# Fewer dummy matmuls, an on-chip broadcast for the last tile, folded output instructions and an early clock warm-up, in an attention + gated-MLP kernel

## Chip, cores, metric

One NeuronCore of one Trainium2 chip. The metric is device time in microseconds (us), median of several executions; lower is better. Engines are called PE (TensorE), ACT (ScalarE), DVE (VectorE), POOL (GpSimd), SP (SyncE, which issues the transfers).

## The reference, cut to what matters

```python
# S = 2048 rows, D = 448, 16 heads of 28, MLP width 1792, all bf16
def reference(x, wqkv, wo, w_gate, w_up, w_down, gate_w):
    g = sigmoid((x * gate_w).sum(-1, keepdims=True))
    q, k, v = split(x @ wqkv)
    a = concat_heads(softmax(q @ k.T * 28 ** -0.5) @ v) @ wo     # attention
    b = (gelu(x @ w_gate) * (x @ w_up)) @ w_down                 # gated MLP
    return g * a + (1 - g) * b
```

## The kernel before

Attention runs in 512 steps: 4 groups of heads, 4 tiles of 512 queries (so 16 tiles, numbered j), two pairs of heads p, 16 blocks of 128 keys. In each step PE computes two score blocks (one pair of heads, each on 32 rows of the array), ACT takes their exponential, and PE multiplies it with V (each head on 32 columns of the array). Between, PE gets "fillers": matmuls of the projections and of the MLP, two a step. Where no real work is ready, dummies are put in.

```python
FILL_BUDGET = [2, 2]
DUMMY_FILL = True
...
def emit_fillers(budget, allow_dummy=True):
    ...
        if j is None:                      # no job ready
            ...
            while n < budget:              # dummies: nobody reads the result
                kb.add("pe", lambda e, _s=dslot: e.matmul(_s.ap[:, 0:512], xT[0][0:128, 0:128],
                                                          xT[0][0:128, 0:512]))
                n += 1
            return
...
for i in range(NSTEP):
    if i + 1 < NSTEP: emit_S(i + 1)        # score pair of the next step
    emit_exp(i)                            # ACT
    emit_fillers((4 if i < EARLY_STEPS else FILL_BUDGET[i % 2]) + extra_fill.get(i, 0))
    emit_PV(i)                             # PV pair
    ...
```

After its 32 steps a tile is divided by the softmax denominators, which lie in one row in 32. For the last tile:

```python
def stage_last():
    Wdve(c_pv, last_pv)
    ... tensor_copy(den_sb, psO[obuf])          # DVE
    ... reciprocal(rrows, den_sb)               # DVE
    ... dma_start(bcast, rows of rrows to all)  # SP: one row to 32 partitions
    ... tensor_tensor(oT, den_sb, bcast, mult)  # DVE
```

Then four tiles of the output are still to be done; each has one matmul and

```python
v1 = tensor_tensor(tmpc[:, t % 2], psum, acc16[:, t], add)
Wdve(c_cb, v1)
if t >= 2: wait(d_out[t - 2])
v2 = scalar_tensor_tensor(outsb[:, t % 2], tmpc[:, t % 2], g16[:, t], b_sb[:, t], mult, add)
... dma_start(out rows, outsb[:, t % 2])
```

The softmax here doesn't subtract the row's maximum and nothing guards it: scores larger than these inputs give would overflow.

## Time and profile before

| | before |
|---|---|
| median (16 runs, with those beside the changed kernel) | 655.5 us |
| span of the profiled run | 654.7 us |
| first real matmul starts | 17.42 |
| first scores start | 30.82 |
| last PV seen complete by DVE | 634.25 |

The four instants cut the run into loading, projections (13.40 us), steps (603.43 us) and tail (20.45 us to the end of the span). They are read from the timeline. The lines themselves stand in the prediction. "Busy" of PE is not work done: matmuls are pipelined, each shows some 0.39 us though a new one can start every 0.216.

### The profile page before, as it was taken

The numbers are of one execution on the slowest core, as the hardware profiler recorded it, in microseconds if no ns is written. First come the engines' busy times: TensorE is split into PE (matmuls) and PEld (weight loads), VectorE is DVE, ScalarE is ACT, GpSimd is POOL, SyncE is SP. The second block draws the span as 40 slices with busy tenths as digits, with TensorE's granted clock in tenths as the row PEclk, the third lists the DMA queues.
The fourth block names the chain that finished last, engine by engine and source line by source line (L and its number), as shares of the span: only waits on it lengthen the run. The fifth ranks groups of instructions, "written<-read, shape, count | busy, mean of one in ns | idle before, by whom it ended". The sixth has DMA issues, their size and how long they took to land.

```text
span 654.7 us, 8803 instructions
## 1 busy us (share of the span) xinstructions
PE 615.3 (94%) x3145; PEld 165.6 (25%) x3145; DVE 311.4 (48%) x603; ACT 541.0 (83%) x542; POOL 11.0 (2%) x22
## 2 busy tenths in 40 slices
PE   0899999999999999999999999999999999999971
PEld 0332222222222222222222222222222222222210
DVE  4553578883154788217874721788111243112053
ACT  0067899999988999999998999999898899889860
POOL 6000000000000000000000000000000000000000
PEclk9999999999999999999999999999999999999995
DMA  8910000000000000000000000000000000100001
GB/s 198 295 29 1 1 18 1 17 2 10 8 2 18 2 17 2 14 5 2 18 1 19 1 17 1 3 17 0 18 1 18 1 10 23 31 10 26 13 28 44
DMA packets 21265, 15.34 MB, mean 23 GB/s; under 512 B 13544, under 2 KB 17832, under 8 KB 21224
## 3 DMA queue, kind: packets, MB, share of 16 engines
q1 hardware_dynamic: 21224, 14.80, 9.4%
q8 instruction: 25, 0.41, 0.3%
q14 instruction: 16, 0.13, 0.1%
HBM read 6.42 MB, written 1.84 MB: 13 GB/s over the span
## 4 chain that ended last, share of the span: by engine, by line
PE 92%; DVE 2%; DMA 2%; SPq 2%; ACT 2%; issue 0%; DVEq 0%
PE psO L792 25%; PE psS L764 25%; PE psY L445 9%; PE psX L445 9%; PE psX L682 6%; PE psY L524 4%; PE psX L524 4%; PE psX L271 2%; PE psY L271 2%; ACT pT L775 2%; SPq L219 1%; DMA bcast<-rrows 1%; PE psS L271 1%; PE psY L563 1%; PE psY L682 1%; PE psX L563 1%
## 5 line engine op out<-in xcount | busy, mean ns | idle before, releaser
L775 ACT ACTIVATE pT<-psS 128x1024 bf16<-128x1024 f32 x512 | 516.1, 1023 | 91.8 <-PE psS L764 76.7
L792 PE MATMUL psO<-pT,vext 128*32 128x512 bf16 x1024 | 201.1, 390 | 2.6 <-ACT pT L775 2.6
L764 PE MATMUL psS<-qT,kT 32*128 32x512 bf16 x1024 | 198.3, 384 | 0.9 <-DVE vext L324 0.9
L792 PEld LDWEIGHTS psO<-pT,vext 128*32 128x32 bf16 x1024 | 49.0, 92 | 206.5 <-issue 171.3
L764 PEld LDWEIGHTS psS<-qT,kT 32*128 32x128 bf16 x1024 | 47.9, 91 | 117.2 <-issue 112.9
L445 PE MATMUL psY<-xT,wg 128*128 128x512 bf16 x224 | 67.8, 384 | 0.0
L445 PE MATMUL psX<-xT,wu 128*128 128x512 bf16 x224 | 65.5, 383 | 0.0
L453 DVE CAST uS<-psX 128x512 bf16<-128x512 f32 x56 | 38.7, 692 | 52.0 <-PE psX L445 52.0
L682 PE MATMUL psX<-xT 128*128 128x512 bf16 x147 | 44.5, 384 | 0.0
L453 DVE CAST gS<-psY 128x512 bf16<-128x512 f32 x56 | 38.5, 688 | 2.7 <-PE psY L445 2.7
L489 DVE SCALAR_TENSOR_TENSOR gu<-gS,uS 128x512 bf16<-128x512 bf16 x56 | 38.3, 684 | 0.0
L513 DVE SCALAR_TENSOR_TENSOR hT<-tt,gu 128x512 bf16<-128x512 bf16 x56 | 35.9, 683 | 1.7 <-ACT tt L501 1.7
L531 DVE TENSOR_SCALAR bsb<-psY,omg 128x448 bf16<-128x448 f32 x8 | 5.5, 684 | 53.7 <-PE psY L524 53.7
L524 PE MATMUL psY<-wd,hT 128*128 128x448 bf16 x112 | 30.9, 358 | 0.0
L524 PE MATMUL psX<-wd,hT 128*128 128x448 bf16 x112 | 30.9, 358 | 0.0
L501 ACT ACTIVATE tt<-zt 128x1024 bf16<-128x1024 bf16 x28 | 29.3, 1048 | 0.0
L531 DVE TENSOR_SCALAR bsb<-psX,omg 128x448 bf16<-128x448 f32 x8 | 5.5, 684 | 41.0 <-PE psX L524 41.0
L483 DVE TENSOR_TENSOR zt<-ww,gS 128x512 bf16<-128x512 bf16 x56 | 23.8, 425 | 2.1
L838 DVE TENSOR_TENSOR oT<-densb,bcast 128x512 bf16<-128x512 f32 x15 | 10.3, 688 | 29.9 <-DMA bcast<-rrows 29.9
L473 DVE TENSOR_TENSOR x<-gS 128x512 bf16<-128x512 bf16 x56 | 23.3, 416 | 0.0
L445 PEld LDWEIGHTS psX<-xT,wu 128*128 128x128 bf16 x224 | 14.6, 98 | 25.6 <-issue 20.4
L587 DVE TENSOR_TENSOR tmpc<-psY,acc 128x448 bf16<-128x448 f32 x8 | 5.0, 624 | 32.2 <-PE psY L577 32.1
(88 smaller groups left out, 258.1 us busy)
## 6 DMA issues: line engine op xcount, KB each, us to landing
bcast<-rrows SPq DMA_DIRECT2D x16, 256.0 KB
out_dram<-outsb SPq DMA_DIRECT2D x16, 112.0 KB, 1.7
wd<-in_B_w_down_dram SPq DMA_DIRECT2D x1, 1568.0 KB, 15.6
wg<-in_B_w_gate_dram SPq DMA_DIRECT2D x3, 448.0 KB, 5.0
wu<-in_B_w_up_dram SPq DMA_DIRECT2D x3, 448.0 KB, 8.4
hT<-in_A_wqkv_dram SPq DMA_DIRECT2D x3, 336.0 KB, 3.5
wop<-in_A_wo_dram SPq DMA_DIRECT2D x16, 24.5 KB
sp<-densb SPq DMA_DIRECT2D x15, 8.0 KB
```

The lines of the kernel that those rows point to most:

```text
L271: return e.matmul(slot.ap[:, 0:512], wsrc[c][0:128, g, :, :], xT[c][0:128, tc * 512:(tc + 1) * 512], start=(c == 0), stop=(c == 3), tile_p ...
L445: e.matmul(s.ap[:, 0:512], _w[_c][0:128, _f * 128:(_f + 1) * 128], xT[_c][0:128, _tc * 512:(_tc + 1) * 512], start=(_c == 0), stop=(_c == ...
L453: v = kb.add("dve", lambda e, _s=s: e.tensor_copy(_dst[:, _k % 2, :], _s.ap[:, 0:512]), ctr=c_d)
L483: kb.add("dve", lambda e, _kp=kp, _mp=mp: e.tensor_tensor(zt[:, _mp, _kp, :], ww[:, :], gS[:, _kp, :], ALU.mult), ctr=c_d)
L489: kb.add("dve", lambda e, _kp=kp, _k4=k % 4: e.scalar_tensor_tensor(gu[:, _k4, :], gS[:, _kp, :], 0.5, uS[:, _kp, :], ALU.mult, ALU.mult), ...
L501: kb.add("act", lambda e, _mp=mp: e.activation(tt[:, :, :], zt[:, _mp, :, :], AF.Tanh, scale=TANH_C), ctr=c_th)
L513: kb.add("dve", lambda e, _kk=kk, _k4=k % 4, _f=f, _tc=tc: e.scalar_tensor_tensor(hT[:, _tc % 2, _f, :], tt[:, _kk, :], 1.0, gu[:, _k4, :] ...
L524: e.matmul(s.ap[:, 0:D], hT[:, _tc % 2, _f, _tl * 128:(_tl + 1) * 128], wd[:, _f, :], start=(_f == 0), stop=(_f == FC - 1), tile_position= ...
L682: kb.add("pe", (lambda e, _s=dslot: e.matmul(_s.ap[:, 0:512], xT[0][0:128, 0:128], xT[0][0:128, 0:512])))
L764: return e.matmul(psS[_buf][:, _hh * 512:(_hh + 1) * 512], kT2[_g % 2][32 * _hp:32 * _hp + 32, _kc * 128:(_kc + 1) * 128], qT2[_g % 2][32 ...
L775: kb.add("act", lambda e, _buf=buf: e.activation(pT[:, _buf, :], psS[_buf][:, 0:1024], AF.Exp, scale=SM_SCALE), ctr=c_exp)
L792: return e.matmul(psO[_obuf][32 * _hp:32 * _hp + 32, :], v_ext[:, _kc, _h, :], pT[:, _buf, _hh * 512:(_hh + 1) * 512], start=(_kc == 0), s ...
```

## The change

It has four parts: (1) where nothing is ready, one dummy a step in place of a full budget; (2) the last tile is normalised in two halves, one per pair of heads, in two PSUM banks, and the reciprocals are spread over partitions by a matmul with a block of ones (`e_bc`) in place of a DMA, with 18 dummies ahead of the second one (a maximum comes before each reciprocal, so that the rows that are no denominators, which the matmul multiplies by 0, stay finite); (3) the gate and the MLP's half are added when the accumulator is evacuated, so that an output tile needs one DVE instruction, with four output buffers; (4) 16 dummies at the start, once the first chunk of the transposed input is there.

```diff
+        kb.wait_sem("pe", d_xt[0], 16)                      # part 4
+        for _ in range(16):
+            kb.add("pe", lambda e: e.matmul(psY[:, 0:512], xT[0][0:128, 0:128], xT[0][0:128, 0:512]))
         Wpe(c_wp, WP_ALL)
...
-                v = ... e.tensor_copy(acc16[:, _t, :], _s.ap[:, 0:D])          # part 3
+                v = ... e.scalar_tensor_tensor(acc16[:, _t, :], _s.ap[:, 0:D],
+                        g16[:, _t:_t + 1], b_sb[:, _t, :], ALU.mult, ALU.add)
...
-                v1 = ... e.tensor_tensor(tmpc[:, _t % 2, :], _s.ap[:, 0:D], acc16[:, _t, :], ALU.add)
-                Wdve(c_cb, v1)
-                if _t >= 2: kb.wait_sem("dve", d_out[_t - 2], 16)
-                v2 = ... outsb[:, _t % 2, :] from tmpc, g16, b_sb
+                if _t >= 4: kb.wait_sem("dve", d_out[_t - 4], 16)
+                v2 = ... e.scalar_tensor_tensor(outsb[:, _t % 4, :], _s.ap[:, 0:D],
+                        g16[:, _t:_t + 1], acc16[:, _t, :], ALU.mult, ALU.add)
...
-                    while n < budget:                                          # part 1
+                    while n < 1:
...
-            def stage_last(): ...                                              # part 2
+        def emit_norm_last(pr, last_pv):      # pr = 0, 1; partitions 64*pr .. 64*pr+63
+            ... tensor_scalar(rrows, den_sb if pr == 0 else psO[obuf], 1e-30, max)
+            ... reciprocal(bcast, rrows)
+            ... (pr == 1: 18 dummies on PE)
+            ... matmul(slot, e_bc, bcast)     # fp32, 64 x 64 tile of the array
+            ... tensor_tensor(oT, den_sb, slot, mult)
```

More of the change, by code (lines that the diff above doesn't have):

```diff
@@ L126, in bass_gated_mix__mha_block__glu_gated_geglu__prompt_kernel @@
         den_sb = T("densb", [128, 512], F32)
+        e_bc = T("ebc", [128, 128], F32)
         sp16 = T("sp16", [128, 16], F32)
@@ L148, in bass_gated_mix__mha_block__glu_gated_geglu__prompt_kernel @@
         omg16 = T("omg16", [128, NT], F32)
-        tmpc = T("tmpc", [128, 2, D], BF16)
-        outsb = T("outsb", [128, 2, D], BF16)
+        outsb = T("outsb", [128, 4, D], BF16)
         psS = [P(f"psS{i}", [128, 1024]) for i in range(2)]
@@ L208, in bass_gated_mix__mha_block__glu_gated_geglu__prompt_kernel @@
         kb.add("pool", lambda e: e.memset(wu[3][0:64, :], 0.0), ctr=c_ms)
+        kb.add("pool", lambda e: e.memset(e_bc[:, :], 0.0), ctr=c_ms)
+        MS_E0 = c_ms.n
+        for hp in range(4):
+            kb.wait("pool", c_ms, MS_E0)
+            kb.add("pool", lambda e, _hp=hp: e.memset(e_bc[32 * _hp:32 * _hp + 1, 32 * _hp:32 * _hp + 32], 1.0), ctr=c_ms)
         MS_ALL = c_ms.n
@@ L568, in evac @@
             def evac(s, _t=t):
-                v = kb.add("dve", lambda e, _s=s: e.tensor_copy(acc16[:, _t, :], _s.ap[:, 0:D]), ctr=c_ae)
+                Wdve(c_be, BE_ALL_holder[0])
+                Wdve(c_g, gate_done["v"])
+                v = kb.add("dve", lambda e, _s=s: e.scalar_tensor_tensor(
+                    acc16[:, _t, :], _s.ap[:, 0:D], g16[:, _t:_t + 1], b_sb[:, _t, :], ALU.mult, ALU.add),
+                    ctr=c_ae)
                 acc_done[_t] = v
@@ L582, in evac @@
                 Wdve(c_ae, acc_done[_t])
-                Wdve(c_be, BE_ALL_holder[0])
-                Wdve(c_g, gate_done["v"])
                 if cb_last[0]:
                     Wdve(c_cb, cb_last[0])
-                v1 = kb.add("dve", lambda e, _s=s: e.tensor_tensor(
-                    tmpc[:, _t % 2, :], _s.ap[:, 0:D], acc16[:, _t, :], ALU.add), ctr=c_cb)
-                Wdve(c_cb, v1)
-                if _t >= 2:
-                    kb.wait_sem("dve", d_out[_t - 2], 16)
-                v2 = kb.add("dve", lambda e: e.scalar_tensor_tensor(
-                    outsb[:, _t % 2, :], tmpc[:, _t % 2, :], g16[:, _t:_t + 1], b_sb[:, _t, :],
+                if _t >= 4:
+                    kb.wait_sem("dve", d_out[_t - 4], 16)
+                v2 = kb.add("dve", lambda e, _s=s: e.scalar_tensor_tensor(
+                    outsb[:, _t % 4, :], _s.ap[:, 0:D], g16[:, _t:_t + 1], acc16[:, _t, :],
                     ALU.mult, ALU.add), ctr=c_cb)
@@ L597, in evac @@
                 kb.add("sp", lambda e: e.dma_start(
-                    out[0, _t * 128:(_t + 1) * 128, :], outsb[:, _t % 2, :]).then_inc(d_out[_t], 16))
-                return (c_cb, v1)
+                    out[0, _t * 128:(_t + 1) * 128, :], outsb[:, _t % 4, :]).then_inc(d_out[_t], 16))
+                return (c_cb, v2)
             j = Job(f"z{t}", mm_fns, evac)
@@ L747, in step_of @@
             return g, qc, p, kc
+        last_j = G * NTC - 1
+        nm_half = {}
+        bc_slot_free = [None]
         def emit_S(i):
@@ L781, in emit_PV @@
             obuf = j % 2
+            if j == last_j and p == 1:
+                obuf = 1 - obuf
             Wpe(c_exp, i + 1)
@@ L786, in emit_PV @@
                 Wpe(c_cp, j - 1)
+            if kc == 0 and p == 1 and j == last_j:
+                Wpe(c_cp, j)
             buf = i % 2
@@ L841, in stage2 @@
                 nm_val[j] = v
-            def stage_last():
-                Wdve(c_pv, last_pv)
-                kb.wait_sem("dve", d_spr, 16 * j)
-                Wdve(c_nm, j)
-                kb.add("dve", lambda e, _obuf=obuf: e.tensor_copy(den_sb[:, :], psO[_obuf][:, :]), ctr=c_cp)
-                cpv = c_cp.n
-                Wdve(c_cp, cpv)
-                kb.wait_sem("dve", d_bc, 16 * j)
-                kb.add("dve", lambda e: e.reciprocal(rrows[:, :], den_sb[:, :]), ctr=c_rc)
-                rcv = c_rc.n
-                Wsp(c_rc, rcv)
-                Wsp(c_nm, j)
-                kb.add("sp", lambda e: e.dma_start(
-                    bcast[:, :], bass.AP(rrows, 0, [[32 * 512, 4], [0, 32], [1, 512]])).then_inc(d_bc, 16))
-                kb.wait_sem("dve", d_bc, 16 * (j + 1))
-                v = kb.add("dve", lambda e, _g=g, _qc=qc: e.tensor_tensor(
-                    oT[_g][:, _qc * 512:(_qc + 1) * 512], den_sb[:, :], bcast[:, :], ALU.mult), ctr=c_nm)
-                nm_step[j] = step[0]
-                nm_val[j] = v
             if j == G * NTC - 1:
-                deferred.append((step[0] + 1, stage_last))
                 return
@@ L868, in emit_norm, with task, copy_out, pe_part @@
             deferred.append((step[0] + 15, stage2))
+        def emit_norm_last(pr, last_pv):
+            g = last_j // NTC
+            qc = last_j % NTC
+            obuf = last_j % 2
+            if pr == 1:
+                obuf = 1 - obuf
+            r0 = 64 * pr
+            def task():
+                Wdve(c_pv, last_pv)
+                if pr == 0:
+                    kb.wait_sem("dve", d_spr, 16 * last_j)
+                    Wdve(c_nm, last_j)
+                def copy_out():
+                    kb.add("dve", lambda e, _o=obuf, _r0=r0: e.tensor_copy(
+                        den_sb[_r0:_r0 + 64, :], psO[_o][_r0:_r0 + 64, :]), ctr=c_cp)
+                    Wdve(c_cp, c_cp.n)
+                if pr == 0:
+                    copy_out()
+                if pr == 0:
+                    kb.wait_sem("dve", d_bc, 16 * last_j)
+                kb.add("dve", lambda e, _r0=r0: e.tensor_scalar(
+                    rrows[_r0:_r0 + 64, :], (den_sb if pr == 0 else psO[obuf])[_r0:_r0 + 64, :], 1e-30, None, ALU.max), ctr=c_rc)
+                Wdve(c_rc, c_rc.n)
+                kb.add("dve", lambda e, _r0=r0: e.reciprocal(bcast[_r0:_r0 + 64, :], rrows[_r0:_r0 + 64, :]), ctr=c_rc)
+                rcv_half[pr] = c_rc.n
+                if pr == 1:
+                    copy_out()
+                if pr == 0:
+                    deferred.append((step[0] + 4, pe_part))
+                else:
+                    pe_part()
+            def pe_part():
+                rcv = rcv_half[pr]
+                slotb = fslots[pr % 2]
+                if slotb.free is not None:
+                    Wpe(slotb.free[0], slotb.free[1])
+                if pr == 1:
+                    for _ in range(18):
+                        kb.add("pe", lambda e, _s=slotb: e.matmul(
+                            _s.ap[:, 0:512], xT[0][0:128, 0:128], xT[0][0:128, 0:512]))
+                Wpe(c_rc, rcv)
+                Wpe(c_ms, MS_ALL)
+                bv = kb.add("pe", lambda e, _s=slotb, _r0=r0: e.matmul(
+                    _s.ap[_r0:_r0 + 64, 0:512], e_bc[_r0:_r0 + 64, _r0:_r0 + 64], bcast[_r0:_r0 + 64, :],
+                    tile_position=(_r0, _r0)), ctr=c_pv)
+                Wdve(c_pv, bv)
+                v = kb.add("dve", lambda e, _s=slotb, _r0=r0: e.tensor_tensor(
+                    oT[g][_r0:_r0 + 64, qc * 512:(qc + 1) * 512], den_sb[_r0:_r0 + 64, :],
+                    _s.ap[_r0:_r0 + 64, 0:512], ALU.mult), ctr=c_nm)
+                nm_half[pr] = v
+                slotb.free = (c_nm, v)
+                slotb.free_step = step[0]
+                if pr == 1:
+                    nm_step[last_j] = step[0]
+                    nm_val[last_j] = v
+            deferred.append((step[0] + 1, task))
@@ L870, in process_deferred @@
+        cp_half = [None]
+        rcv_half = {}
         def process_deferred():
@@ L888, in bass_gated_mix__mha_block__glu_gated_geglu__prompt_kernel @@
                 emit_norm(g * NTC + qc, c_pv.n)
+            if g * NTC + qc == last_j and kc == KC - 1:
+                emit_norm_last(p, c_pv.n)
             process_deferred()
```

## The prediction

> **What bounds the kernel now.** I read the page's first two parts first, then the chain that ended last in order of time, then the timeline at both ends. The page's head and its clock row say that TensorE (PE) is the engine to think about, and that its clock is full except in the last slice:
>
> ```profile
> PE 615.3 (94%) x3145; PEld 165.6 (25%) x3145; DVE 311.4 (48%) x603; ACT 541.0 (83%) x542; POOL 11.0 (2%) x22
> PEclk9999999999999999999999999999999999999995
> ```
>
> The middle of the chain, in order of time (start, us, piece), shows one attention step as a cycle on PE:
>
> ```profile
> 605.11 0.32 PE psO L792 x2
> 605.43 0.32 PE psS L764 x2
> 605.75 0.54 PE psX L682 x2
> 606.29 0.32 PE psO L792 x2
> ```
>
> A step is a pair of PV matmuls (L792), a pair of score matmuls (L764) and two fillers: 0.32 + 0.32 + 0.54 = 1.18 us. Here the fillers are dummies of L682, which compute nothing. Neighbouring matmuls of one kind start 0.216 us apart (the 16 warm ones below), so two take 0.43 and 0.11 goes to changing the array's tiling; the pairs, which run beside each other, cost 0.216 + 0.11 each. ScalarE (ACT) is not far behind. Where fillers are few, its exponentials run back to back, and there the chain changes to ACT (timeline: start, us, engine, group; then two PV rows of that stretch):
>
> ```profile
> 31.25 2.86 ACT L775 ACTIVATE pT<-psS 128x1024 bf16<-128x1024 f32 x3 [29.22 <-PE psS L764]
> ...
> 625.73 0.39 PE L792 MATMUL psO<-pT,vext 128*32 128x512 bf16 x2 [0.18 <-ACT pT L775]
> ...
> 629.42 0.39 PE L792 MATMUL psO<-pT,vext 128*32 128x512 bf16 x2 [0.18 <-ACT pT L775]
> ```
>
> Three exponentials of 1.02 in 2.86 us start (2.86-1.02)/2 = 0.92 apart; from 625.73 to 629.42 are four steps of 0.92. So ACT's floor is 0.92 us a step, PE's with two fillers 1.18.
>
> The two ends are serial (timeline of the first 31 us, and of the last 21):
>
> ```profile
> 4.85 10.12 SPq L219 DMA_TRANSPOSE xT<-in_A_x_dram  x4
> 17.42 1.86 PE L271 MATMUL psS<-xT,wqP 128*128 128x512 bf16 x4 [17.42 <-DMA xT<-in_A_x_dram]
> 23.68 1.03 PE L271 MATMUL psO<-xT,wkP 128*128 128x512 bf16 x4
> 30.82 0.60 PE L764 MATMUL psS<-qT,kT 32*128 32x512 bf16 x4 [0.94 <-DVE vext L324]
> 634.25 0.69 DVE L847 COPY densb<-psO 128x512 f32<-128x512 f32 x1 [4.28 <-PE psO L792]
> 634.98 3.35 DVE L851 RECIPROCAL rrows<-densb 128x512 f32<-128x512 f32 x1
> 645.29 0.69 DVE L858 TENSOR_TENSOR oT<-densb,bcast 128x512 bf16<-128x512 f32 x1 [6.96 <-DMA bcast<-rrows]
> 646.13 0.53 PE L577 MATMUL psY<-wop,oT 128*128 128x448 bf16 x1 [11.92 <-DVE oT L858]
> 651.79 0.69 DVE L592 SCALAR_TENSOR_TENSOR outsb<-tmpc,g,bsb 128x448 bf16<-128x448 bf16 x1
> ```
>
> At the start the first 16 projection matmuls take 6.43 us on the chain (17.42 to 23.85, 0.40 each) and the next four 0.86 (0.216 each): the first are cold. At the end, after the last PV (634.25), come copy, reciprocal, a 6.9 us DMA broadcast, multiply, and four output tiles each of two VectorE (DVE) instructions in series; the span ends at 654.7, so this tail is 20.4 us.
>
> **What the Trainium skill says.** "TensorE: Matmul & The Clock Gate", section "What's actually happening": PE runs at half clock until it has been busy for a window of about 3.4 us, with a free-running window. The trace agrees in direction (0.40 then 0.216 us) but shows 5 to 6 us of cold work. "TensorEngine Tiling (Array Packing)", "Key Properties": changing the tiling mode drains the array. The trace shows 0.11 us at each change; so one filler costs 0.216 + 0.11, and removing the second saves only 0.216. "VectorE: DVE Perf Modes", "The TRN2 errata": an fp32 tensor_tensor takes (N+151)/0.96 ns, 691 for 512; L858 agrees at 0.69. I use it to say that 64 partitions in place of 128 save no time. "FP8 and Floating Point Precision", "TensorE Precision Notes": true FP32 is four passes. No matmul in this trace is fp32; the new one I estimate at 4 x 0.216 = 0.86 us plus some 0.2 for drain.
>
> **Part 1, one dummy a step in place of two.** The order of both built programs' instructions, cut into the 512 steps at the PV pairs, gives: 80 steps with two dummies keep one; one step with four keeps one; three with one output matmul and one dummy lose the dummy; one loses both to the new broadcast matmul. 169 dummies become 81. All else in the steps is the same, in the same order. A step with one dummy has PE work of 3 x 0.32 = 0.966 us, still just above ACT's 0.92. The rest of its loop fits: scores start to exponential start is 0.43 us (624.22 to 624.65), the exponential 1.02, some 0.05 to the PV, 1.50 in all, where PE reaches that PV only five thirds of a cycle, 1.61 us, after the scores. So PE stays the bound, by little, and 80 x 0.216 = 17.3 us is saved. The three mixed steps fall from about 1.16 to the ACT floor, 3 x 0.2 = 0.6. The four-dummy step stands at a Tanh (1.05 us on ACT): two PE steps of 1.18 + 1.61 = 2.79 against three ACT instructions at 0.92 to 0.95, some 2.8; it and its neighbour gain nothing, -0.2. Sum 17.7.
>
> **Part 2, the last tile's normalisation in halves.** The first half's VectorE work (copy 0.69, maximum about 0.5, reciprocal 3.35, near 4.6 with gaps) starts after step 495 and lies beside four to five steps of 0.966; its broadcast matmul comes after PV of step 500, about 5.1 us later, so hardly a wait. The matmul is 0.86 to 1.0 us plus an added tiling change, in a step that loses two dummies of 0.54: about 0.5 us lost. The second half is the tail, counted from the last PV: maximum from PSUM 0.70, reciprocal to 4.1, broadcast matmul (0.86 + 0.2, the 18 dummies before it last 18 x 0.216 = 3.9 us and keep it warm without delaying it) to 5.3, multiply to 6.05; the copy of 0.69 hides beside the matmul. The first output matmul then gives its result by 6.6. Before, the same point (646.70) was at 12.45. Saved 5.85.
>
> **Part 3, one VectorE instruction per output tile.** Before, four tiles take 646.70 to 652.49 = 5.8 us, 1.48 a tile for the first three. After, one instruction of 0.69 and a wait between, 0.72: 4 x 0.72 = 2.9. Saved 2.9. The other instruction is not gone, it is folded into the accumulator's evacuation (0.625 becomes 0.685, 16 times), where VectorE idles between tiles. Four output buffers remove a wait that cost nothing (0.6 us of idle in all). The last store's 2.2 us stay. So the tail is 6.6 + 2.9 + 2.2 = 11.7 in place of 20.4: 8.7 saved in parts 2 and 3.
>
> **Part 4, 16 dummies at the start.** They wait only for the first transposed chunk, issued at 4.85 and landed 5.2 us later, at 10.05. Cold at 0.43 they end at 16.9, with some warm earlier; the real work begins at 17.42 as before, since the last chunk is still what it waits for. Then 16 matmuls take 3.46 us in place of 6.43; VectorE, at 0.87 a V tile against PE's 0.86, can follow. Saved 2.7 (estimate), if the gap of about 1 us does not cool the clock. The five added GpSimd memsets come after those that anything early waits for.
>
> **Sum.** 17.7 - 0.5 + 8.7 + 2.7 = 28.6. From 655.4: 626.8 us.
>
> **The rivals.** (a) The dummies' steps fall to ACT's floor: 80 x 0.04 = 3.5 us more, 623. For it: the drain could be partly overlapped where PE waits. Against it: the chain's 0.11 is in every cycle. (b) PE and ACT, now nearly equal, wait for each other in turn, and a step takes 1.02 (the exponential's full length) rather than 0.966: 80 x 0.05 = 4.3 us back, 631. For it: both buffers are only two deep; against it: exponentials 0.92 apart exist. (c) The dummies were what kept the clock full, and half as many let it fall: each dummy step would go to about 1.7 us or more, 80 x 0.7 = 56 us, some 680. Against it: stretches with one or no filler (624.8 to 630) keep matmuls at 0.39 and the clock row at 9. (d) The early dummies do not warm it, or overrun: the 2.7 is lost, 629.5. (e) The fp32 matmul or the DVE queue at step 500 stalls PE for longer: 2 us, 629.
>
> **Range and chances.** (a), (b), (d) and (e) together are some 5 us either way; a little more upwards, since more of them cost. Low 621, high 632. Faster by over 2% means under 642.3; only (c) or an error in several parts at once would miss that: faster 0.97, same 0.02, slower 0.01.
>
> **What would show it.** Right: the chain's cycle in the last third of the run reads 0.32, 0.32, 0.32 and the L689 dummies number about 81 (97 with the first, 115 with all); matmuls at 17.4 start 0.216 apart; no DMA between the last PV and the last store's; the tail from the last PV 11 to 12.5 us; the broadcast matmul about 1 us. Wrong: a dummy step of 0.92 or 1.02; granted clock under 0.9 in the last third; ACT idle time ended by the broadcast matmul over 1.5 us; VectorE waiting at the start for matmuls spaced 0.43.

## The result, and the profile after

| | before | after |
|---|---|---|
| median | 655.5 us (16 runs) | 628.57 us (8 runs, 628.05 to 629.03) |
| ratio | | 0.9588, 95% interval 0.9579 to 0.9597 |
| loading, to the first real matmul | 17.42 | 16.34 |
| projections, to the first scores | 13.40 | 10.59 |
| steps, to the last PV | 603.43 | 586.79 |
| tail, to the end of the span | 20.45 | 12.08 |

A ratio here is the mean time of one kernel's fast runs over that of the other's of the same rounds, so not quite the ratio of the medians quoted. The spans differ by 28.9 us, the medians by 26.9: the profile of before happens to have late input (17.42) and a long cold phase, that of after early input.

First the page of the changed kernel: PE, and its clock in 40 slices.

```profile
PE 605.3 (97%) x3095; PEld 167.5 (27%) x3095; DVE 308.5 (49%) x592; ACT 536.1 (86%) x542; POOL 11.5 (2%) x27
PEclk9999999999999999999999999999999999999998
```

The clock is full from end to end. The chain that ended last (start, us, piece), in the stretch of dummies, answers to the cycle shown of before:

```profile
580.61 0.32 PE psX L689
580.93 0.32 PE psO L807 x2
581.25 0.32 PE psS L775 x2
581.57 0.32 PE psX L689
581.89 0.32 PE psO L807 x2
```

The filler piece went from 0.54 to 0.32, the step from 1.18 to 0.96, and it is still PE that is followed, not ACT. The start (timeline: start, us, engine, group):

```profile
4.87 9.14 SPq L224 DMA_TRANSPOSE xT<-in_A_x_dram  x4
9.57 6.24 PE L269 MATMUL psY<-xT 128*128 128x512 bf16 x16 [9.57 <-DMA xT<-in_A_x_dram]
16.34 1.02 PE L279 MATMUL psS<-xT,wqP 128*128 128x512 bf16 x4 [0.53 <-DMA xT<-in_A_x_dram]
26.93 0.61 PE L775 MATMUL psS<-qT,kT 32*128 32x512 bf16 x4 [0.94 <-DVE vext L332]
```

The dummies take the cold phase, beside loads that the real work waits for anyway; the first four real matmuls now take 1.02 us in place of 1.86. The tail (timeline):

```profile
613.72 0.69 DVE L886 TENSOR_SCALAR rrows<-psO 64x512 f32<-64x512 f32 x1 [4.32 <-PE psO L807]
614.45 3.35 DVE L889 RECIPROCAL bcast<-rrows 64x512 f32<-64x512 f32 x1
617.86 1.07 PE L909 MATMUL psY<-bcast,ebc 64*64 64x512 f32 x2 [0.18 <-DVE bcast L889]
619.03 0.69 DVE L913 TENSOR_TENSOR oT<-densb,psY 64x512 bf16<-64x512 f32 x1 [0.69 <-PE psY L909]
620.26 0.68 DVE L599 SCALAR_TENSOR_TENSOR outsb<-psX,g,acc 128x448 bf16<-128x448 f32 x1 [0.53 <-PE psX L589]
621.14 0.68 DVE L599 SCALAR_TENSOR_TENSOR outsb<-psY,g,acc 128x448 bf16<-128x448 f32 x1 [0.20 <-DVE outsb L599]
622.91 0.68 DVE L599 SCALAR_TENSOR_TENSOR outsb<-psY,g,acc 128x448 bf16<-128x448 f32 x1 [0.20 <-DVE outsb L599]
```

No DMA stands between the last PV and the last store. The broadcast is a matmul of 1.07 us (one fp32 matmul, two records) in place of 6.91. The output instructions start 0.885 apart, with 0.20 of idle before each.

What part 2 costs before the tail is seen at step 500, where the first half's broadcast matmul stands between the score and PV pairs:

```profile
602.42 1.07 PE L909 MATMUL psX<-bcast,ebc 64*64 64x512 f32 x2
603.85 9.38 ACT L786 ACTIVATE pT<-psS 128x1024 bf16<-128x1024 f32 x10 [0.92 <-PE psS L775]
```

ACT idles 0.92 us for it.

### The profile page after: what moved, and what is told of

Same layout as the page of the kernel before. It is cut to its first block, busy times and chain, and to the rows that moved or that the text cites. A ratio compares the mean times of both kernels' runs of the same rounds, so it can differ in the third digit from the quotient of the medians.

```text
span 625.8 us, 8697 instructions
## 1 busy us (share of the span) xinstructions
PE 605.3 (97%) x3095; PEld 167.5 (27%) x3095; DVE 308.5 (49%) x592; ACT 536.1 (86%) x542; POOL 11.5 (2%) x27
## 4 chain that ended last, share of the span: by engine, by line
PE 92%; ACT 2%; DVE 2%; SPq 2%; issue 1%; DMA 1%; DVEq 0%; ACTq 0%
PE psO L807 26%; PE psS L775 25%; PE psY L453 10%; PE psX L453 9%; PE psY L532 4%; PE psX L532 4%; PE psX L689 3%; PE psX L279 2%; PE psY L279 2%; ACT pT L786 2%; SPq L224 1%; PE psY L571 1%; PE psX L571 1%; PE psY L285 1%; PE psX L285 1%
## 5 line engine op out<-in xcount | busy, mean ns | idle before, releaser
L689 PE MATMUL psX<-xT 128*128 128x512 bf16 x70 | 27.3, 390 | 0.0
L453 PEld LDWEIGHTS psY<-xT,wg 128*128 128x128 bf16 x224 | 12.8, 98 | 25.4 <-issue 25.4
```

Source lines behind the costliest of these rows:

```text
L453: e.matmul(s.ap[:, 0:512], _w[_c][0:128, _f * 128:(_f + 1) * 128], xT[_c][0:128, _tc * 512:(_tc + 1) * 512], start=(_c == 0), stop=(_c == ...
L689: kb.add("pe", (lambda e, _s=dslot: e.matmul(_s.ap[:, 0:512], xT[0][0:128, 0:128], xT[0][0:128, 0:512])))
```

## The experiments

All gave correct results. Each ran beside the kernel before on one chip; "against the change" is the difference of its ratio from 0.9588, times 655.5 us, so it carries the uncertainty of both, 0.6 to 1 us. An execution over 1.5% above the fastest of its kernel counts as slow; there were three, one in e5 and two in e10. The runs are called e1 to e12. The stage times of the profiles are steadier: the steps stage of the five runs that differ elsewhere only (the change, e2, e3, e6, e9) lasted 586.79 to 586.80.

**One part undone at a time.** Part 1 (e1):

```diff
-                    while n < 1:
+                    while n < budget:
```

> The changed kernel with two dummies a step again (part 1 alone undone). Theory (PE sets the step, a second dummy costs its own 0.216 us and no tiling change): 80 steps go from 0.966 back to 1.18 us, about +17 us, so some 645.5 us; the cycle reads 0.32, 0.32, 0.54. Rival (the saving came from a PE-ACT coupling that the other parts also remove): clearly less than +14 us.

Measured 645.94 us, ratio 0.9861 (0.9848 to 0.9875), +17.9 against the change. Projections 10.59, steps 604.16, tail 12.0. The chain reads as expected:

```profile
603.04 0.54 PE psX L689 x2
603.58 0.32 PE psO L807 x2
603.90 0.32 PE psS L775 x2
```

The steps stage is 17.37 longer, 0.217 for each of 80 steps: the time of one more matmul. The rival falls. And against the kernel before (603.43), which has the same dummies but no broadcast matmul in the steps, it is 0.73 longer: that is the price of part 2 at step 500.

Part 4 (e2):

```diff
-        kb.wait_sem("pe", d_xt[0], 16)
-        for _ in range(16):
-            kb.add("pe", lambda e: e.matmul(psY[:, 0:512], xT[0][0:128, 0:128], xT[0][0:128, 0:512]))
```

> The changed kernel without the 16 dummies before the first projection. Theory (they warm the clock beside the transposing loads): the first 16 real matmuls take 6.4 us in place of 3.5 and the first scores come 2.8 us later after the first real matmul; +2.7 to +3.0 us, so some 631.4. Rival (the earlier start of the real work in the profile of the changed kernel, 16.3 against 17.4 us, came from the dummies too): +3.9 us, and the first real matmul back at 17.4.

Measured 630.58 us, ratio 0.9622 (0.9609 to 0.9635), +2.2. Its start (timeline):

```profile
16.32 1.86 PE L277 MATMUL psS<-xT,wqP 128*128 128x512 bf16 x4 [16.32 <-DMA xT<-in_A_x_dram]
21.23 1.03 PE L277 MATMUL psO<-xT,wkP 128*128 128x512 bf16 x4
28.38 0.61 PE L773 MATMUL psS<-qT,kT 32*128 32x512 bf16 x4 [0.94 <-DVE vext L330]
```

The input came at 16.32 without the dummies, and in other runs with them at 17.4 and 17.5: the early input was chance, the rival falls. The size is not a constant. The first 16 matmuls took 4.91 us here and 6.26 in the profile of before (17.42 to 23.68). With 0.427 cold (six of the early dummies' weight loads in the changed kernel's trace start from 10.40 to 12.96) and 0.216 warm that is some 7 and 13 cold ones. So the early dummies were worth 1.47 us in this profile (projections 12.06 against 10.59) and 2.81 against that of before, 2.2 in the mean of the runs.

Part 3 (e3):

```diff
-        outsb = T("outsb", [128, 4, D], BF16)
+        tmpc = T("tmpc", [128, 2, D], BF16)
+        outsb = T("outsb", [128, 2, D], BF16)
 ...    # accumulator: plain copy; output: add, wait, scalar_tensor_tensor, as before
```

> The changed kernel with two VectorE instructions per output tile and two output buffers again (part 3 alone undone). Theory: from the first output matmul's result to the last evacuation 5.8 us in place of 3.35, so +2.4 us, 631.0. Rival (the wait instructions before each output instruction take what the fold saved): under +1.5 us.

Measured 630.82 us, ratio 0.9632 (0.9619 to 0.9646), +2.9. Projections and steps to the hundredth as in the change (10.59, 586.79), tail 14.56 in place of 12.08: +2.48, as expected; so the fold saves all of it in the tail, and nothing in the steps.

Part 2 (e4):

```diff
+            def stage_last(): ...        # copy, reciprocal, DMA broadcast, multiply, as before
 ...    # and the last tile in one PSUM bank, as before
-            if g * NTC + qc == last_j and kc == KC - 1:
-                emit_norm_last(p, c_pv.n)
```

> The changed kernel with the last tile's broadcast by DMA again (part 2 alone undone; the 18 dummies before the broadcast matmul go with it). Theory: the tail up to the first output matmul is 11.9 us in place of 6.15 (+5.7), the output matmul is cold (+0.2), and the 0.7 us that the first half's broadcast matmul cost in step 500 come back: +5.2 us, 633.8. Rival (most of the halving is worth nothing since the second half alone is as long as the whole): the same sum if only the DMA matters, but then the loss should equal the DMA's 6.9 us less the broadcast matmul's 1.1.

Measured 633.6 us, ratio 0.9676 (0.9663 to 0.9689), +5.8. Tail 18.05, +5.97; steps 585.84, -0.95; together +5.0. The two theories give near the same sum here, as was said, so this run confirms the size and doesn't part them; the tail's loss is the DMA's 6.91 less the matmul's 1.08, and the output matmul cold by 0.2. The halving itself (one half's reciprocal ahead of the end) was not tried alone; the tail's reciprocal still takes 3.35 us on 64 partitions, as it took on 128, so halving by partitions did not shorten it. Term by term the tail of before and after differs by the broadcast, not by the halving; the first half's matmul costs 0.73 to 0.95 in the steps (e1, this run). One broadcast matmul for the whole tile at the end would leave that out, as an estimate from these figures; it was not run, and no run has a matmul of that shape.

The four losses by stages are 17.37, 2.81 (with the cold phase of before), 2.48 and 5.02, 27.7 in all; before and after differ in the same stages by 27.8. The 2.81 stands on both sides; what the sum tests is the other three, 24.87 against 25.01 in steps and tail. These parts add.

**No dummies in the steps (e5).** Is one a step needed?

```diff
-DUMMY_FILL = True
+DUMMY_FILL = False
```

> The changed kernel with no dummies in the steps at all (those at the start and the 18 in the tail stay). Theory (the last dummy and its tiling change keep PE just above ACT's floor; the clock does not need it, since score and PV pairs alone keep PE busy 0.64 of 0.92 us): the steps fall from 0.966 to 0.92 us, 80 x 0.04 = -3.5 us, some 625.0, granted clock 0.99 as before. Rival (the dummy is what keeps the clock full): matmuls of 0.7 us and more in the last third, steps over 1.2 us, +20 us or more.

Measured 659.76 us (654.41 to 665.45), ratio 1.0032: 29 us slower than the change, granted clock 0.887 to 0.911 in all six runs. My theory fell, the rival holds. The busy time in stretches (stretch, length, PE busy (x), then PEld, DVE, ACT, POOL, PE clock, DMA share, GB/s):

```profile
440.00:460.00 20.00, 17.57 (x92) 4.62 (x90) 14.49 (x28) 18.52 (x21) 0.00 (x0) 0.94 0.02 3
480.00:500.00 20.00, 20.00 (x106) 5.25 (x104) 2.22 (x4) 17.56 (x18) 0.00 (x0) 0.97 0.02 3
600.00:640.00 40.00, 39.56 (x138) 7.38 (x136) 9.50 (x11) 33.06 (x33) 0.00 (x0) 0.50 0.07 20
```

Between 600 and 640 PE is busy 39.56 of 40 us, at half clock, with score and PV pairs but for four output matmuls and the broadcast, and does not recover; between 480 and 500 it is back at full, some 15 us after full-array fillers of the down projection set in (466.4), and later falls again. So PE's busy share alone does not bring the clock back; full-array matmuls supply something that the pairs, whose matmuls use 32 rows or 32 columns each, don't. What it is was not tested. The chain around the drop:

```profile
450.24 0.97 PE psX L453 x4
454.80 0.39 PE psO L807 x2
458.49 0.61 PE psO L807 x2
459.64 0.54 PE psO L807 x2
460.18 0.54 PE psS L775 x2
```

The last full fillers end at 451.2; the pairs turn slow some 6 us later. Here PE also idled, about a quarter of the time (busy 4.06 us from 452.0 to 457.4), so the drop alone does not part idle time from the kind of matmul; the stretch of e8 shown below bears on that. The prediction had argued that the clock was safe from the stretch of 624.8 to 630: that is 5 us, with an output matmul in every other step, too short to say so.

**Half-length dummies (e10).**

```diff
-    e.matmul(_s.ap[:, 0:512], xT[0][0:128, 0:128], xT[0][0:128, 0:512])
+    e.matmul(_s.ap[:, 0:256], xT[0][0:128, 0:128], xT[0][0:128, 0:256])
```

> The changed kernel with the dummies in the steps half as long (256 columns; those at the start and in the tail as they are). The run without any lost the clock, though PE was busy 70 to 96% of the time by the score and PV pairs. Theory (a modest share of full-array work is enough): the clock stays at 0.99 and the step falls to ACT's floor of 0.92, -3.5 us, 625.0. Rival (what counts is the full-array work in a window, and 0.107 us in a step is too little): clock under 0.95 and over 635 us.

Four runs of the same program: 624.97, 629.92, 638.56 and 644.19 us, at clocks 0.997, 0.985, 0.969 and 0.961 (the ratio 0.9677, 0.9599 to 0.9754, is that of all four). The first two count as fast; even they differ by the clock. The profile is of the first, and its chain shows the step that the theory promised:

```profile
563.44 0.38 PE psO L807 x2
563.82 0.32 PE psS L775 x2
564.14 0.21 PE psX L689
564.35 0.38 PE psO L807 x2
```

A step is 0.92 us, ACT's floor. (ACT's busy share does not show it: from 560 to 600 us it is 40.00 of 40 here and in the change.) So both expectations are met in part, in different executions, though no clock fell under the rival's 0.95: the floor is worth 3.6 us where the clock holds (one run, 624.97 against 628.57; its steps stage is 583.06 against 586.79), and at half the full-array work the clock holds only sometimes. The change's one full dummy a step, with clocks of 0.996 to 0.998 in all its runs, is the least amount in every step tried that was safe.

**Tail dummies (e6).**

```diff
-                    for _ in range(18):
+                    for _ in range(0):
```

> The changed kernel without the 18 dummies before the last broadcast matmul. Theory (they only keep the clock): PE idles some 4 us, the broadcast matmul is cold, 1.9 us in place of 1.08, and the first output matmul 0.55 in place of 0.36; the later ones hide beside VectorE: +1.0 us, 629.5. Rival (4 us of idle are too short to lose the clock here): no difference over 0.3 us.

Measured 629.74 us, ratio 0.9599 (0.9584 to 0.9615). The ratios differ by less than their intervals, but the stages settle it: steps equal (586.80), tail 13.13 in place of 12.08. The broadcast matmul took 1.98 in place of 1.08, the first output matmul 0.55 in place of 0.36. The theory holds: +1.05.

**Broadcast in bf16 (e7).**

```diff
-        e_bc = T("ebc", [128, 128], F32)
+        e_bc = T("ebc", [128, 128], BF16)
+        rbf = T("rbf", [128, 512], BF16)      # the reciprocals, in place of bcast
```

> The changed kernel with the reciprocals and the ones of the broadcast matmul in bf16, so one pass in place of four. Theory: the matmul falls from 1.08 to about 0.45 us (0.216 + drain) in the tail, and from 1.00 to 0.3 in step 500: -0.6 and -0.5, so some 627.4. Rival (the 1.08 us is mostly fixed latency, not passes): under 0.3 us in all. Right within tolerance.

Measured 627.33 us, ratio 0.9563 (0.9548 to 0.9578), correct. Steps 586.14 (-0.65), tail 11.38 (-0.70). The matmul in the tail (timeline):

```profile
618.25 0.40 PE L910 MATMUL psY<-rbf,ebc 64*64 64x512 bf16 x1 [0.19 <-DVE rbf L890]
```

1.08 (the chain's figure) against 0.40 is 0.68 less, about three times 0.216, as if three of four passes were saved. That agrees with "FP8 and Floating Point Precision", "TensorE Precision Notes", which gives four passes for true FP32.

**Fewer waits before the output instructions (e9).** This takes up the one term of the tail that was off, 0.885 per output tile in place of 0.72.

```diff
-                Wdve(c_ae, acc_done[_t])
-                if cb_last[0]:
-                    Wdve(c_cb, cb_last[0])
+                if not cb_last[0]:
+                    Wdve(c_ae, c_ae.n)        # once, for all accumulators
```

> The changed kernel with one wait for all accumulators ahead of the first output instruction, and without each output instruction's wait for the one before it (other buffers, same engine). The prediction gave 0.72 us per output tile, the profile shows 0.885. Theory (each further wait costs VectorE's sequencer some 0.05 to 0.1 us, in series with the instructions): the last four evacuations start 0.72 to 0.80 apart, tail 0.3 to 0.5 us shorter, 628.1. Rival (the 0.2 us gap belongs to the instruction's own drain): still 0.885 apart.

Measured 627.83 us, ratio 0.9579 (0.9564 to 0.9593): alone no clear difference in time. In the profile the tail is 11.19 in place of 12.08 (timeline):

```profile
621.24 0.68 DVE L598 SCALAR_TENSOR_TENSOR outsb<-psX,g,acc 128x448 bf16<-128x448 f32 x1 [0.53 <-PE psX L589]
621.84 0.67 DVE L598 SCALAR_TENSOR_TENSOR outsb<-psY,g,acc 128x448 bf16<-128x448 f32 x1
622.43 0.67 DVE L598 SCALAR_TENSOR_TENSOR outsb<-psX,g,acc 128x448 bf16<-128x448 f32 x1
```

0.60 apart, even less than the 0.68 of one: without the wait for its forerunner an instruction starts before that one has ended. The theory holds in direction and was too timid: the waits cost 0.29 a tile. The two waits were taken away together, so how it splits between them stays open.

**Fillers in lumps (e8).** If a change of tiling costs 0.106 us, two groups of two fillers should cost one change more than one group of four.

```diff
-FILL_BUDGET = [2, 2]
+FILL_BUDGET = [4, 0]
```

> The changed kernel with four fillers in every other step and none between, in place of two in each; same work. Theory (0.106 us is paid for each change of tiling, so three changes a step; joining the fillers saves one change in two steps): a pair of steps takes 2.25 in place of 2.36 us; 176 pairs, -19 us; dummy steps fall to ACT's floor, -3.5: some 606 us, 603 to 612. Rival (0.106 is not the change of tiling but part of each group's waits, or ACT starves while PE does four fillers): no gain, or slower than 628.

Measured 628.76 us (625.39, 625.88, 631.64, 631.68), clocks 0.986, 0.987, 0.975, 0.975; ratio 0.9582 (0.9545 to 0.9619). No gain in the median. The two runs at the higher clock are some 3 us faster than the change; the profile is of one of them, with steps of 584.07 against 586.79. By the profile the gain was lost in two ways: the clock fell in part (with a budget of none, every other dummy step has no dummy), and the MLP stretch became longer. Two rows of the timeline for each kernel, first the change, then this one, Tanh instructions on ACT:

```profile
81.79 1.05 ACT L509 ACTIVATE tt<-zt 128x1024 bf16<-128x1024 bf16 x1
99.85 1.05 ACT L509 ACTIVATE tt<-zt 128x1024 bf16<-128x1024 bf16 x1
```

```profile
80.48 1.05 ACT L509 ACTIVATE tt<-zt 128x1024 bf16<-128x1024 bf16 x1
99.81 1.05 ACT L509 ACTIVATE tt<-zt 128x1024 bf16<-128x1024 bf16 x1
```

Two Tanh periods took 18.06 us, here 19.33: 0.63 a period more, and there (80 to 100 us) 39% of this kernel's chain is ACT's exponentials and Tanh, where the change's is PE alone. Two stretches of dummy steps and fillers in the same profile (columns as above):

```profile
470.00:500.00 30.00, 30.00 (x146) 8.60 (x145) 3.19 (x6) 24.09 (x25) 0.00 (x0) 0.84 0.05 10
560.00:600.00 40.00, 36.29 (x196) 10.30 (x194) 9.63 (x12) 40.00 (x44) 0.00 (x0) 1.00 0.08 21
```

From 560 to 600 PE is busy 36.29 of 40 us, less than the 39.56 at half clock in e5, and the clock is full: with a full-array dummy or output matmul in every other step, idle time of that size need not lose it. But at 466 it was lost, with a dummy in every other step too and PE busy 4.62 us of the 6 before; whether idle time or the want of full-array work did that stays open. To test the cost of a change of tiling without these, lumps only where down- and output-projection fillers stand (e11):

```diff
+            nxt = pick_job()
+            lump = nxt is not None and nxt.kind in ("a", "b")
-            emit_fillers((4 if i < EARLY_STEPS else FILL_BUDGET[i % len(FILL_BUDGET)]) + extra_fill.get(i, 0))
+            emit_fillers((4 if i < EARLY_STEPS else (4, 0)[i % 2] if lump else 2) + extra_fill.get(i, 0))
```

> The changed kernel with four and none fillers in turn only where the fillers are down-projection or output-projection matmuls (272 of them, 136 steps, no Tanh beside them), two in each step elsewhere. Theory (a change of tiling costs 0.106 us, and the run with four and none everywhere lost its gain at the Tanh instructions and to the clock): 68 changes fewer, -7.2 us, 621.3, clock 0.99. Rival (there is no such gain, or the clock falls here too): 627 or more.

Measured 622.97 us, ratio 0.9502 (0.9488 to 0.9517), clock 0.996 to 0.997. The chain of two such steps:

```profile
469.46 0.86 PE psX L532 x4
470.32 0.32 PE psO L807 x2
470.65 0.32 PE psS L775 x2
470.96 0.32 PE psO L807 x2
471.29 0.32 PE psS L775 x2
471.61 0.86 PE psX L532 x4
```

A pair of steps takes 2.15 us; with two fillers in each it is 2 x 1.13 = 2.26. So joining saves 0.11 per pair, as the cost of a change of tiling says. The steps stage is 580.87, -5.9 us; 68 pairs would make -7.2, and the missing 1.3 us I did not trace. The starts of the exponentials show where it lies: in each of the first three stretches of down-projection fillers (56 matmuls, 14 pairs of steps) a tile's 32 steps take 34.92 us in place of 36.38, 1.46 less, where 14 x 0.106 is 1.48; the shortfall is in the last five tiles, and the last alone takes 0.58 more. That the 0.11 goes with the tiling and not with any new group of matmuls is seen where two groups of full-array matmuls, with other weights and another bank, follow each other: their starts lie 0.44 us apart for two matmuls (e8's trace, 454.35 and 454.79).

**Together (e12).**

```diff
 e11_lump_ba + e7_bf16_broadcast + e9_fewer_waits
```

> The changed kernel with the three gains together: four and none fillers where they are down- or output-projection matmuls, the broadcast matmul in bf16, fewer waits before the output instructions; one full dummy a step as in the change. Theory: the gains lie in different stages and add: -5.6 for the fillers, -1.2 for bf16, -0.6 for the waits, as measured one by one: some 621.2 us, clock 0.99. Rival (they overlap, or the tail is set by something else by then): no better than 622.5.

Measured 620.48 us, ratio 0.9459 (0.9446 to 0.9472), clock 0.997, correct. Steps 580.20, tail 10.69 (against 586.79 and 12.08). In the steps the gains add (6.59 against 5.92 and 0.65), in the tail nearly (1.39 against 0.70 and 0.89): the last output matmuls, 0.36 each in the change, take 0.46 and 0.55 here. This beats both kernels, the change by 1.3%.

## Why the prediction was right

*PE sets the dummy steps, and the second dummy costs 0.216.* Right, in mechanism and size, given that the clock held: step 0.966, 81 dummies in the trace, 17.4 us by undoing it alone.

*The first half costs 0.5 at step 500.* Right in kind, 0.73 in size: the matmul took 1.0 on the chain as expected, but ACT idled 0.92.

*The tail to the first output result, 6.6.* It took 6.54, with the reciprocal, the 1.08 matmul and the multiply at the expected places. *2.9 for the four output tiles* was the term most off: 0.885 apart in place of 0.72, 3.3 in all. I had counted one semaphore wait per instruction, where the program has up to four; e9, which takes two of them away, shows that they were it.

*Early dummies, 2.7.* The mechanism holds. The size was taken from one profile whose cold phase was a long one; over runs it was 2.2.

*626.8 against 628.6.* The terms named make 0.2 + 0.4 + 0.5, and part 1 gave 17.4 where its sum said 17.7; these 1.4 of the 1.8 us are accounted for, and the rest is within the runs' spread.

*Rival (a), ACT's floor,* is real (e10's first run) but the change stays 0.04 above it. *(b)* did not occur. *(e)* occurred in small, 0.2 us more than expected at step 500; of *(d)* nothing is seen, since the early dummies end at 15.81, before the input at 16.34, and the real matmuls start warm. *Rival (c), the clock,* did not strike this change, but its refutation was wrong: without dummies the loss is 29 us, and half of one is not safe. That one dummy a step was enough was luck, since the prediction had no figure for how much is needed. The 0.97 for "faster" was better than the argument under it.

Two slips in the working: the "16 warm ones below" are four in the lines shown, and the step's distance from ACT's floor, 0.966 - 0.92 = 0.046, is rounded to 0.04 in the product that gives 3.5 (it makes 3.7).

## What to carry to other kernels

When a filler is removed, ask what its group costs and what its members cost: the group carries the change of tiling, each further member only its own time, and a removal pays back only where that engine sets the step. Before removing work that seems to do nothing, undo it wholly in one run and look at the granted clock: one dummy a step was nearly free and needed, two were waste. In a serial tail count waits, passes and transfers one by one, as each is visible there; and compare stages between profiles, not spans, where loading alone moves by a microsecond.

## What the Trainium skill lacked or had wrong

- "TensorE: Matmul & The Clock Gate", section "What's actually happening", says the clock follows how busy PE has been. Here PE was busy 39.56 of 40 us with pairs on 32 rows or 32 columns, at clock 0.50 (e5); full-array matmuls of 0.216 us in each step of 0.966 held it at 0.997, of 0.107 in 0.92 only sometimes (0.961 to 0.997, e10). Of matmuls on part of the array the page says nothing like this. In e8 a busy share of 36.29 of 40 us came with clock 1.00.
- "TensorEngine Tiling (Array Packing)", "Key Properties", says that a change of tiling mode drains the array, but not what it costs: 0.106 us in every cycle of these traces, and 0.11 regained per change left out (e11).
- "VectorE: DVE Perf Modes", "The DRAIN you can't avoid", says that chaining without semaphores does not skip the wait for an empty pipe, and that a semaphore cost nothing extra in its test; it also says that an instruction that is not held starts earlier, which fits e9. The first part does not fit: here instructions of 0.68 us started 0.60 apart without the wait for the one before and for the accumulator, and 0.885 apart with both (e9).
